# Memory rows of the weight gradients transposed inside their own stage, and the last 64 channels of two column groups computed side by side

## The chip, the cores and the metric

The kernel runs on one core of one Trainium2 chip, in one launch. The metric is the device time of that launch in microseconds (us), the median of several runs. The profile is one execution taken by the hardware profiler. PE is TensorE's matmuls, PEld its weight loads, DVE the vector engine, ACT the scalar engine, POOL GpSimd, SP the engine that only issues transfers. L79 is line 79 of the kernel, a helper that records all matmuls, so PE is read by tile names.

One measure is used throughout: the **stage**, the time from the end of the last matmul of the x gradients to the end of the span, read from each run's trace. Each stage time is that of one profile, and how well it repeats was not measured as such.

## The reference, cut to what matters

The reference is the forward pass and all gradients of a gated sum of two attentions: A, multi-query, and B, recurrent over 64 segments of 32 tokens with 8 memory rows.

```
def _B_ref(x, mem0, Wq, Wk, Wv, Wo, seg_len):       # x (1,2048,576), 32 heads of 128
    mem = mem0                                       # 8 rows
    for s in range(n_seg):                           # 64 segments
        h = concat([mem, x[segment s]])              # 8 + 32 rows
        q, k, v = h@Wq, h@Wk, h@Wv                   # per head
        o = softmax(mask(q k^T * scale)) v
        o = o @ Wo
        mem = o[:8]; outs.append(o[8:])
    return concat(outs)
...
_out, _vjp = jax.vjp(_f, ...)
return (_out, *_vjp(grad_out))
```

The last stage of the kernel forms the weight gradients of B: dWq, dWk and dWv (576 x 4096 each) are h^T times dq, dk, dv, and dWo (4096 x 576) is o^T times dy. The sum runs over 2560 rows: 2048 tokens and 64 x 8 = 512 memory rows, which is 16 + 4 blocks of 128. Of the 576 channels, four blocks have 128 and the fifth has 64.

## The kernel before: the parts that matter

The token rows of dq, dk, dv and o lie in DRAM in token order. The memory rows come out of the recurrence in another order, transposed, so a stage of its own turns them and writes them to DRAM:

```python
def b_mem_rows(self, sp, psum):
    for mt in range(self.NM // P):                     # 4 blocks x 4 sources
        for src, wi, dst in ((self.ME, 3, self.OM), (self.DME, 1, self.DM["q"]), ...):
            raw = sp.tile([P, 16, 256], BF16, name="m_raw", bufs=2)
            nc.sync.dma_start(raw[:], src[16 * mt:16 * mt + 16, :, wi, :]...)
            hm = sp.tile([P, HB, 16, MEM], BF16, name="m_hm", bufs=2)
            ...                                        # 16 copies bring the rows into order
            tk = sp.tile([P, 2, 4, 4, E], BF16, name="m_tk", bufs=2)
            for ri in range(8):
                self.tr4(psum, "x_tr", ..., tk[:, ri // 4, :, ri % 4, :])   # 4 transposes, 1 copy
            nc.gpsimd.dma_start(dst[mt * P:(mt + 1) * P, :], tk[:]...)
```

Then the weight gradient stage loads h, dy and one column group (512 of 4096 columns) after another, and multiplies:

```python
        def columns(xsrc, msrc, jc):
            t = sp.tile([P, NH, 512], BF16, name="w_col", bufs=2)
            for q in range(0, NTT, 4):
                (nc.sync if q % 8 == 0 else nc.gpsimd).dma_start(t[:, q:q + 4, :], xsrc[:, cs]...)
            nc.sync.dma_start(t[:, NTT:NH, :], msrc[:, cs]...)
            return t
        ...                                            # gate product, 32 matmuls
        for w, oi in (("q", 7), ("k", 8), ("v", 9)):
            for jc in range(8):
                t = columns(self.DX[w], self.DM[w], jc)
                for kt in range(NKT):                  # 5 channel blocks: 128,128,128,128,64
                    acc = psum.tile([P, 512], F32, name="w_acc", bufs=3)
                    for n in range(NH):                # 20 row blocks
                        self.mm(acc[0:rows, :], lhsT=h[:, n, kt * P:kt * P + rows], rhs=t[:, n, :], ...)
                    ...                                # copy to SBUF, store
        ...                                            # output gradient: 8 groups
```

The softmax here doesn't subtract the row's maximum and nothing guards it: scores larger than these inputs give would overflow.

## Time and profile before

| | before |
|---|---|
| median of 4 runs | 8813.72 us (8796.3 to 8819.1) |
| stage (end of x gradients to end) | 831.1 us |
| of that, until the first weight gradient matmul | 144.6 us |
| q, k, v gradients | 526.1 us |
| output gradient | 157.0 us |
| end | 3.5 us |

The page of the kernel before has the busy share of each engine, then the span in 40 equal slices of 220 us (a 9 is 90% or more; PEclk is the granted TensorE clock in tenths):

```profile
PE 8158.4 (93%) x89816; PEld 3903.5 (44%) x89816; DVE 4321.7 (49%) x6659; ACT 3835.0 (44%) x7412; POOL 1184.8 (13%) x3062
...
PEclk9999999999999989979999999989999877776999
DMA  2000000000000045542211588883333466666444
...
DMA packets 615950, 969.83 MB, mean 110 GB/s; under 512 B 187545, under 2 KB 406946, under 8 KB 594850
```

The stage is the last four slices.

### The profile page before, as it was taken

The numbers are of one execution on the slowest core, as the hardware profiler recorded it, in microseconds if no ns is written. First come the engines' busy times: TensorE is split into PE (matmuls) and PEld (weight loads), VectorE is DVE, ScalarE is ACT, GpSimd is POOL, SyncE is SP. The second block draws the span as 40 slices with busy tenths as digits, with TensorE's granted clock in tenths as the row PEclk, the third lists the DMA queues.
The fourth block names the chain that finished last, engine by engine and source line by source line (L and its number), as shares of the span: only waits on it lengthen the run. The fifth ranks groups of instructions, "written<-read, shape, count | busy, mean of one in ns | idle before, by whom it ended". The sixth has DMA issues, their size and how long they took to land. (4 is left out here: it accounts for less than half of the span.)

```text
span 8801.6 us, 210293 instructions
## 1 busy us (share of the span) xinstructions
PE 8158.4 (93%) x89816; PEld 3903.5 (44%) x89816; DVE 4321.7 (49%) x6659; ACT 3835.0 (44%) x7412; POOL 1184.8 (13%) x3062
## 2 busy tenths in 40 slices
PE   6999999999999979978999899979999799997999
PEld 2222222222222234435555566647777555554444
DVE  4889898898888924432333455542222111113000
ACT  3788787787777823332222355542222111112000
POOL 4100001000010014420000133320000011112000
PEclk9999999999999989979999999989999877776999
DMA  2000000000000045542211588883333466666444
GB/s 89 1 6 1 6 6 1 6 1 6 6 1 1 1 146 230 231 178 86 60 59 59 175 267 263 260 284 104 99 98 97 167 189 190 185 187 221 149 149 144
DMA packets 615950, 969.83 MB, mean 110 GB/s; under 512 B 187545, under 2 KB 406946, under 8 KB 594850
## 3 DMA queue, kind: packets, MB, share of 16 engines
q1 hardware_dynamic: 540978, 672.32, 24.4%
q0 software_dynamic: 72720, 282.73, 8.6%
q8 instruction: 702, 11.50, 0.5%
q14 instruction: 238, 1.95, 0.1%
q10 hardware_dynamic: 1312, 1.33, 0.0%
HBM read 552.06 MB, written 404.10 MB: 109 GB/s over the span
## 5 line engine op out<-in xcount | busy, mean ns | idle before, releaser
L1355 DVE TENSOR_TENSOR a_U<-a_d,a_E 128x1024 bf16<-128x1024 f32 x2048 | 2474.3, 1224 | 302.3 <-ACT a_E L1350 233.1
L1350 ACT ACTIVATE a_E<-a_s 128x512 bf16<-128x512 f32 x4096 | 2237.5, 595 | 564.7 <-PE a_s L79 478.9
L79 PE MATMUL a_s<-a_qaug,a_kmask 128*128 128x512 bf16 x2048 | 704.1, 388 | 54.7 <-ACT a_tk L1432 24.5
L79 PE MATMUL a_s<-a_kmask,a_qaug 128*128 128x512 bf16 x2048 | 697.3, 384 | 25.9 <-ACT a_E L1350 9.6
L79 PE MATMUL w_acc<-w_col,w_h 128*128 128x512 bf16 (+1 forms) x2400 | 526.1, 381 | 0.9 <-DMA w_col<-dqx 0.9
L79 PEld LDWEIGHTS <-d_g 128*32 128x32 bf16 x18432 | 494.6, 97 | 26.4 <-issue 9.9
L63 DVE CAST p_tok<-p_pb 128x512 bf16<-128x512 f32 x384 | 265.3, 692 | 318.4 <-PE p_pb L79 318.4
L79 PE MATMUL a_d<-a_doT,a_vaugT 32*128 32x512 bf16 x2048 | 401.5, 389 | 0.1
L79 PE MATMUL a_d<-a_vaugT,a_doaT 32*128 32x512 bf16 x2048 | 397.6, 385 | 0.0
L65 ACT COPY p_em<-p_tr 128x512 bf16<-128x512 bf16 x384 | 225.0, 586 | 357.7 <-PE p_tr L84 357.5
L1442 POOL TENSOR_TENSOR a_otok<-a_tk,a_rl 128x144 bf16<-128x144 f32 x64 | 27.5, 429 | 2525.4 <-DVE a_rl L1441 2525.4
L79 PEld LDWEIGHTS <-w_h 128*128 128x128 bf16 (+1 forms) x2400 | 237.4, 100 | 289.4 <-issue 24.2
L79 PEld LDWEIGHTS <-a_vaugT 32*128 32x128 bf16 x2048 | 96.4, 91 | 572.7 <-issue 572.6
L79 PEld LDWEIGHTS <-a_doaT 32*128 32x128 bf16 x2048 | 95.9, 91 | 538.0 <-issue 537.6
L65 ACT CAST c_tm<-c_pb 128x512 bf16<-128x512 f32 x192 | 112.5, 586 | 471.4 <-PE c_pb L79 471.2
L1042 ACT ACTIVATE g_dt<-x_p 128x512 bf16<-128x512 f32 x256 | 142.7, 599 | 355.5 <-DMA dvx<-g_dt 216.0
L63 DVE CAST c_tm<-c_pb 128x512 bf16<-128x512 f32 x192 | 132.9, 692 | 313.6 <-PE c_pb L79 309.2
L63 DVE CAST w_o<-w_acc 128x512 bf16<-128x512 f32 (+1 forms) x60 | 41.4, 690 | 481.3 <-PE w_acc L79 448.6
L79 PEld LDWEIGHTS <-c_mT 128*32 128x32 bf16 x7680 | 187.9, 96 | 190.9 <-DVE c_mT L396 25.4
L79 PEld LDWEIGHTS <-a_kmask 128*128 128x128 bf16 x2048 | 125.1, 97 | 313.8 <-issue 305.9
L79 PEld LDWEIGHTS <-p_xT 128*128 128x128 bf16 (+1 forms) x1920 | 154.8, 97 | 218.0 <-issue 87.7
L65 ACT CAST w_o<-w_acc 128x512 bf16<-128x512 f32 (+1 forms) x60 | 35.1, 585 | 496.6 <-PE w_acc L79 496.6
(482 smaller groups left out, 13797.5 us busy)
## 6 DMA issues: line engine op xcount, KB each, us to landing
xt_k<-p_tok SPq DMA_DIRECT2D x16, 1024.0 KB, 4.0
xe_k<-p_em POOLq DMA_DIRECT2D x16, 1024.0 KB, 5.5
xs_k<-p_seg POOLq DMA_DIRECT2D x64, 256.0 KB, 4.3
xt_v<-p_tok SPq DMA_DIRECT2D x16, 1024.0 KB, 3.9
xe_v<-p_em POOLq DMA_DIRECT2D x16, 1024.0 KB, 5.6
xs_v<-p_seg POOLq DMA_DIRECT2D x64, 256.0 KB, 2.9
xt_q<-p_tok SPq DMA_DIRECT2D x16, 1024.0 KB, 4.2
xe_q<-p_em POOLq DMA_DIRECT2D x16, 1024.0 KB, 5.8
```

The lines of the kernel that those rows point to most:

```text
L63: nc.vector.tensor_copy(out, in_)
L65: nc.scalar.copy(out, in_)
L79: self.follow(self.nc.tensor.matmul(out, lhsT, rhs, start=start, stop=stop, tile_position=tp, skip_group_check=True))
L1042: nc.scalar.mul(dt[:, g], pk[:], sc)
L1350: nc.scalar.activation(ex[:, j, :], s[:, :], ACT.Exp, scale=SCALEA)
L1355: nc.vector.tensor_tensor(out=u[:], in0=d[:], in1=ex[:], op=ALU.mult)
L1442: nc.gpsimd.tensor_tensor(out=osl, in0=v[:, :, :, o0:o0 + DA], in1=rl[:].to_broadcast([P, 4, 2, DA]), op=ALU.mult)
```

## The change

Its intent is to do away with the stage of memory rows: the raw rows are loaded to SBUF as they lie, four copies per column group bring them into order, and PE transposes them straight into the column group's buffer, inside the stage that PE bounds. At the same time the 64-channel block is done for two column groups at once, one in each half of the array. A third w_col buffer is needed for that, and everything is issued two groups ahead.

```diff
-    def b_mem_rows(self, sp, psum):          # the whole stage, its DRAM buffers and its call
 ...
+        def load_raw(w):
+            raw = raws[w] = sp.tile([P, self.NSEG, 256], BF16, name="w_raw", bufs=2)
+            for s in range(0, self.NSEG, 16):
+                nc.gpsimd.dma_start(raw[:, s:s + 16, :], src[s:s + 16, :, wi, :]...)
+        def columns(w, jc):
-            t = sp.tile([P, NH, 512], BF16, name="w_col", bufs=2)
+            t = sp.tile([P, NH, 512], BF16, name="w_col", bufs=3)
             for q in range(0, NTT, 4):
+                nc.sync.dma_start(t[:, q:q + 4, :], xsrc[:, cs]...)
-            nc.sync.dma_start(t[:, NTT:NH, :], msrc[:, cs]...)
+            hm = sp.tile([P, 4, self.NSEG, MEM], BF16, name="w_hm", bufs=2)
+            for i in range(4):
+                (nc.gpsimd if i == 3 else nc.vector).tensor_copy(hm[:, i], raws[w][:, :, c0:c0 + MEM])
+            for mt in range(NMT):
+                ptr = psum.tile([P, 4, P], BF16, name="w_tr", bufs=2)
+                for i in range(4):
+                    self.tr(ptr[:, i, :], hm[:, i, 16 * mt:16 * mt + 16, :]..., P)
+                nc.scalar.copy(t[:, NTT + mt, :], ptr[:]...)
 ...
+        load_raw("q")
+        t0 = columns("q", 0)
+        ...                                   # dy loads, rows of h and dy, then columns("q", 1)
+        def projection(od, jc, t, t2):
+            if jc % 2 == 0:                   # 64 channels of two column groups
+                acc = bank("w_acc64", 2)
+                for n in range(NH):
+                    for x, tx in enumerate((t, t2)):
+                        self.mm(acc[64 * x:64 * x + 64, :], lhsT=h[:, n, 512:D], rhs=tx[:, n, :], ..., tp=(0, 64 * x))
+            for kt in range(4): ...           # as before
 ...
+        for n, (w, jc) in enumerate(order):
+            if jc == 0 and w != "o":
+                load_raw("qkvo"["qkvo".index(w) + 1])
+            if n + 2 < len(order):
+                ts.append(columns(*order[n + 2]))
+            ...                               # projection or output of group n
+            if n == 0: gate()
```

The output gradient keeps its 1280 matmuls, but its last 64 columns go to a bank of their own.

More of the change, by code (lines that the diff above doesn't have):

```diff
@@ L176, in setup_dram @@
         self.OX = DT([T, J], "ox")
-        self.OM = DT([NM, J], "om")
     def load_B_fwd(self, pool):
@@ L773, in setup_dram_bwd @@
         self.DX = {"q": self.DQX, "k": DT([T, J], "dkx"), "v": DT([T, J], "dvx")}
-        self.DM = {w: DT([NM, J], f"dm_{w}") for w in "qkv"}
     def b_transpose_weights(self, sp, psum):
@@ L1055, in b_x_gradients @@
             nc.sync.dma_start(self.outs[1][tok, :], dx[:])
-    def b_mem_rows(self, sp, psum):
-        nc = self.nc
-        for mt in range(self.NM // P):
-            for src, wi, dst in ((self.ME, 3, self.OM), (self.DME, 1, self.DM["q"]), (self.DME, 2, self.DM["k"]), (self.DME, 3, self.DM["v"])):
-                raw = sp.tile([P, 16, 256], BF16, name="m_raw", bufs=2)
-                nc.sync.dma_start(raw[:], src[16 * mt:16 * mt + 16, :, wi, :].rearrange("s p n -> p s n"))
-                hm = sp.tile([P, HB, 16, MEM], BF16, name="m_hm", bufs=2)
-                for s in range(16):
-                    (nc.gpsimd if s % 2 else nc.vector).tensor_copy(hm[:, :, s, :], raw[:, s].rearrange("p (h m) -> p h m", m=MEM))
-                tk = sp.tile([P, 2, 4, 4, E], BF16, name="m_tk", bufs=2)
-                for ri in range(8):
-                    self.tr4(psum, "x_tr", lambda g: hm[:, 4 * ri + g].rearrange("p s m -> p (s m)"), tk[:, ri // 4, :, ri % 4, :])
-                nc.gpsimd.dma_start(dst[mt * P:(mt + 1) * P, :], tk[:].rearrange("p r g i e -> p (r g i e)"))
     def b_weight_gradients(self, keep, sp, psum):
@@ L1079, in b_weight_gradients @@
             nc.sync.dma_start(h[:, q:q + 4, :], self.A_x.rearrange("(n p) d -> p n d", p=P)[:, q:q + 4, :])
-            nc.sync.dma_start(dy[:, q:q + 4, :], self.db_dram[:, :].rearrange("(n p) d -> p n d", p=P)[:, q:q + 4, :])
         def rows_of(dst, hist, c0):
             for k4, n in ((0, 4), (4, 1)):
-                ptr = psum.tile([P, 4, P], BF16, name="w_tr", bufs=1)
+                ptr = psum.tile([P, 4, P], BF16, name="w_tr", bufs=2)
                 for k in range(n):
@@ L1090, in rows_of @@
                 self.evac(dst[:, k4 * P:k4 * P + w], ptr[:].rearrange("p k n -> p (k n)")[:, 0:w])
+        raws = {}
+        def load_raw(w):
+            src, wi = (self.ME, 3) if w == "o" else (self.DME, 1 + "qkv".index(w))
+            raw = raws[w] = sp.tile([P, self.NSEG, 256], BF16, name="w_raw", bufs=2)
+            for s in range(0, self.NSEG, 16):
+                nc.gpsimd.dma_start(raw[:, s:s + 16, :], src[s:s + 16, :, wi, :].rearrange("s p n -> p s n"))
+        def columns(w, jc):
+            xsrc = self.OX if w == "o" else self.DX[w]
+            t = sp.tile([P, NH, 512], BF16, name="w_col", bufs=3)
+            cs = slice(jc * 512, (jc + 1) * 512)
+            for q in range(0, NTT, 4):
+                nc.sync.dma_start(t[:, q:q + 4, :], xsrc[:, cs].rearrange("(n p) c -> p n c", p=P)[:, q:q + 4, :])
+            hm = sp.tile([P, 4, self.NSEG, MEM], BF16, name="w_hm", bufs=2)
+            for i in range(4):
+                c0 = ((jc // 4) * 16 + i * 4 + jc % 4) * MEM
+                (nc.gpsimd if i == 3 else nc.vector).tensor_copy(hm[:, i], raws[w][:, :, c0:c0 + MEM])
+            for mt in range(NMT):
+                ptr = psum.tile([P, 4, P], BF16, name="w_tr", bufs=2)
+                for i in range(4):
+                    self.tr(ptr[:, i, :], hm[:, i, 16 * mt:16 * mt + 16, :].rearrange("p s m -> p (s m)"), P)
+                nc.scalar.copy(t[:, NTT + mt, :], ptr[:].rearrange("p i n -> p (i n)"))
+            return t
+        load_raw("q")
+        t0 = columns("q", 0)
+        for q in range(0, NTT, 4):
+            nc.sync.dma_start(dy[:, q:q + 4, :], self.db_dram[:, :].rearrange("(n p) d -> p n d", p=P)[:, q:q + 4, :])
         for mt in range(NMT):
@@ L1097, in b_weight_gradients @@
         nc.sync.dma_start(self.outs[6].rearrange("b m d -> (b m) d"), dm0[0:MEM, :])
-        def columns(xsrc, msrc, jc):
-            t = sp.tile([P, NH, 512], BF16, name="w_col", bufs=2)
-            cs = slice(jc * 512, (jc + 1) * 512)
-            for q in range(0, NTT, 4):
-                (nc.sync if q % 8 == 0 else nc.gpsimd).dma_start(t[:, q:q + 4, :], xsrc[:, cs].rearrange("(n p) c -> p n c", p=P)[:, q:q + 4, :])
-            nc.sync.dma_start(t[:, NTT:NH, :], msrc[:, cs].rearrange("(n p) c -> p n c", p=P))
-            return t
+        bank = lambda name, bufs: psum.tile([P, 512], F32, name=name, bufs=bufs)
@@ L1107, in b_weight_gradients @@
         dz16 = keep.tile([P, NTT], BF16, name="w_dz16")
         nc.vector.tensor_copy(dz16[:], self.dz_all[:])
-        pg = psum.tile([P, 640], F32, name="w_acc2", bufs=2)
-        for lo, hi in ((0, 512), (512, D)):
-            for n in range(NTT):
-                self.mm(pg[0:1, lo:hi], lhsT=dz16[:, n:n + 1], rhs=h[:, n, lo:hi], start=(n == 0), stop=(n == NTT - 1))
         dg16 = keep.tile([1, D], BF16, name="w_dgate16")
-        nc.vector.tensor_copy(dg16[:, :], pg[0:1, 0:D])
-        nc.sync.dma_start(self.outs[11][None, :], dg16[:, :])
@@ L1116, in b_weight_gradients @@
-        for w, oi in (("q", 7), ("k", 8), ("v", 9)):
-            od = self.outs[oi].rearrange("d h e -> d (h e)")
-            for jc in range(8):
-                t = columns(self.DX[w], self.DM[w], jc)
-                for kt in range(NKT):
-                    rows = KT_ROWS[kt]
-                    acc = psum.tile([P, 512], F32, name="w_acc", bufs=3)
-                    for n in range(NH):
-                        self.mm(acc[0:rows, :], lhsT=h[:, n, kt * P:kt * P + rows], rhs=t[:, n, :], start=(n == 0), stop=(n == NH - 1))
-                    o16 = sp.tile([P, 512], BF16, name="w_o", bufs=3)
-                    self.evac(o16[0:rows, :], acc[0:rows, :])
-                    nc.sync.dma_start(od[kt * P:kt * P + rows, jc * 512:(jc + 1) * 512], o16[0:rows, :])
@@ L1128, in b_weight_gradients, with gate @@
-        oo = self.outs[10].rearrange("h e d -> (h e) d")
-        for jc in range(8):
-            t = columns(self.OX, self.OM, jc)
+        order = [(w, jc) for w in "qkvo" for jc in range(8)]
+        ts = [t0, columns(*order[1])]
+        def gate():
+            for lo, hi in ((0, 512), (512, D)):
+                pg = bank("w_acc", 4)
+                for n in range(NTT):
+                    self.mm(pg[0:1, 0:hi - lo], lhsT=dz16[:, n:n + 1], rhs=h[:, n, lo:hi], start=(n == 0), stop=(n == NTT - 1))
+                nc.vector.tensor_copy(dg16[:, lo:hi], pg[0:1, 0:hi - lo])
+            nc.sync.dma_start(self.outs[11][None, :], dg16[:, :])
@@ new lines, in projection @@
+        def projection(od, jc, t, t2):
[3 more added lines that the diff above has]
+                    for x, tx in enumerate((t, t2)):
+                        self.mm(acc[64 * x:64 * x + 64, :], lhsT=h[:, n, 512:D], rhs=tx[:, n, :], start=(n == 0), stop=(n == NH - 1), tp=(0, 64 * x))
+                o16 = sp.tile([P, 512], BF16, name="w_o", bufs=3)
+                self.evac(o16[:, :], acc[:, :])
+                for x in range(2):
+                    nc.sync.dma_start(od[512:D, (jc + x) * 512:(jc + x + 1) * 512], o16[64 * x:64 * x + 64, :])
+            for kt in range(4):
+                acc = bank("w_acc", 4)
+                for n in range(NH):
+                    self.mm(acc[:, :], lhsT=h[:, n, kt * P:(kt + 1) * P], rhs=t[:, n, :], start=(n == 0), stop=(n == NH - 1))
+                o16 = sp.tile([P, 512], BF16, name="w_o", bufs=3)
+                self.evac(o16[:, :], acc[:, :])
+                nc.sync.dma_start(od[kt * P:(kt + 1) * P, jc * 512:(jc + 1) * 512], o16[:, :])
@@ L1131, in b_weight_gradients, with output @@
+        def output(oo, jc, t):
+            a64 = bank("w_acc64", 2)
             for i in range(4):
-                acc = psum.tile([P, 640], F32, name="w_acc2", bufs=2)
+                acc = bank("w_acc", 4)
                 for n in range(NH):
-                    for lo, hi in ((0, 512), (512, D)):
-                        self.mm(acc[:, lo:hi], lhsT=t[:, n, i * E:(i + 1) * E], rhs=dy[:, n, lo:hi], start=(n == 0), stop=(n == NH - 1))
-                o16 = sp.tile([P, D], BF16, name="w_oo", bufs=3)
@@ L1137, in b_weight_gradients @@
-                self.evac(o16[:, :], acc[:, 0:D])
-                j0 = jc * 512 + i * E
-                nc.sync.dma_start(oo[j0:j0 + E, :], o16[:, :])
+                    lt = t[:, n, i * E:(i + 1) * E]
+                    self.mm(acc[:, :], lhsT=lt, rhs=dy[:, n, 0:512], start=(n == 0), stop=(n == NH - 1))
+                    self.mm(a64[:, 64 * i:64 * i + 64], lhsT=lt, rhs=dy[:, n, 512:D], start=(n == 0), stop=(n == NH - 1))
+                o16 = sp.tile([P, 512], BF16, name="w_o", bufs=3)
@@ new lines, in output @@
+                self.evac(o16[:, :], acc[:, :])
+                j0 = jc * 512 + i * E
+                nc.sync.dma_start(oo[j0:j0 + E, 0:512], o16[:, :])
+            o64 = sp.tile([P, 4, 64], BF16, name="w_o64", bufs=2)
+            self.evac(o64[:], a64[:, 0:256].rearrange("p (i c) -> p i c", i=4))
+            nc.sync.dma_start(oo[jc * 512:(jc + 1) * 512, 512:D].rearrange("(i p) c -> p i c", p=P), o64[:])
+        for n, (w, jc) in enumerate(order):
[3 more added lines that the diff above has]
+                ts.append(columns(*order[n + 2]))
+            if w == "o":
+                output(self.outs[10].rearrange("h e d -> (h e) d"), jc, ts[n])
+            else:
+                projection(self.outs[{"q": 7, "k": 8, "v": 9}[w]].rearrange("d h e -> d (h e)"), jc, ts[n], ts[n + 1])
+            if n == 0:
+                gate()
@@ L1649, in build_full @@
                     k.b_x_gradients(p5k, p5s, p5p)
-            with SB("p5m") as p5m, PS("p5mp") as p5mp:
-                k.b_mem_rows(p5m, p5mp)
             with SB("p6k") as p6k, SB("p6s") as p6s, PS("p6p") as p6p:
```

## The prediction

> **What bounds the kernel now.** I read the page first: PE is busy 93% of the span, but the slices just before the last three show DMA at 8 and a granted clock of 7. So I cut the end of the run into stages, with the busy time, the granted clock and the DMA share of each (columns: stretch, its length, busy us and instruction count of PE, PEld, DVE, ACT, POOL, then PEclk, DMA share, GB/s):
>
> ```profile
> 7970.50:8090.70 120.20, 68.84 (x516) 54.11 (x517) 54.30 (x194) 37.50 (x64) 53.31 (x144) 0.51 0.91 281
> 8090.70:8115.06 24.36, 14.95 (x73) 6.50 (x73) 4.46 (x11) 1.92 (x9) 3.02 (x4) 0.50 0.92 303
> 8115.06:8641.10 526.04, 526.04 (x2400) 237.32 (x2399) 41.38 (x60) 34.50 (x59) 34.36 (x46) 0.99 0.45 147
> 8641.10:8798.20 157.10, 157.02 (x1281) 80.63 (x1280) 12.12 (x16) 10.22 (x17) 10.46 (x14) 1.00 0.45 147
> ```
>
> The first row is the memory row stage. No engine is full, PE runs at half clock, and the DMA share is 0.91: transfers bound it. It lasts 120.2 us, from the last matmul of the x gradients to the landing of the last row block. The second row is the opening of the weight gradients, again transfers. The last two rows (q, k, v gradients, then the output gradient) are PE alone: 526.04 busy in 526.04 us at full clock, with transfers at half load. The chain of waits that ended last says the same of the seam:
>
> ```profile
> 8086.26 4.14 DMA dm_v<-m_tk
> ...
> 8093.07 15.63 DMA w_h<-in_A_x_dram
> ...
> 8110.19 0.37 SPq L1097
> 8110.56 0.06 issue
> 8110.61 4.41 DMA w_col<-dqx
> 8115.02 0.04 issue
> 8115.06 683.07 PE w_acc L79 x3680
> 8798.13 0.02 issue
> 8798.16 0.64 ACT w_oo L65
> ```
>
> Nothing of the last stage loads before the last row block lands (8090.40). Then h, and after it the first column group. L1097 is the small store of the memory gradient: SP takes its queue in order, so the first SP load of w_col stands behind it. From 8115.06 nothing but matmuls is on the path.
>
> **What the Trainium skill says.** (1) "TensorEngine Tiling (Array Packing)", When to Use Tiling: a stationary operand of 64 columns allows two column tiles, up to twice the rate. Its Key Properties add that a change of tiling mode drains TensorE. The trace of before supports the first with tiles of 32 columns (columns: start, us, what):
>
> ```profile
> 4401.95 1.05 PE L79 MATMUL c_pb<-Wq,c_mT 128*32 128x512 bf16 x16 [0.30 <-DVE c_mT L396]
> 4402.83 0.39 PE L79 MATMUL c_pb<-Wqk,c_mT 128*32 128x512 bf16 x4
> 4403.04 1.04 PE L79 MATMUL c_pb<-Wq,c_mT 128*32 128x512 bf16 x16
> ```
>
> Twenty matmuls of 512 columns pass from 4401.95 to 4403.04, 1.09 us: 0.218 us for each set of four. The drain is not seen on its own. (2) "TensorE: Matmul & The Clock Gate", Wait — 56ns, not 53.3ns?: 215.7 ns from start to start for 512 columns warm, 55.6 for 128. The trace agrees: 80 full matmuls in 17.38 us (217 ns), and the transposes below. (3) "DMA: Bandwidth & Descriptors", Queues, rings and completion order: an engine takes its queues in turn, a packet at a time. In before, POOL's w_col loads go in packets of 4096 B (four 1024 B rows that land side by side), SP's in 1024 B; median times 159 and 46 ns in the packet records. So where both queues have work, POOL gets most of the bytes.
>
> **The change part by part.** *Removed, transfers:* the memory rows are no longer written to DRAM in token order (16 stores of 1 MB) nor read back (32 loads of 512 KB), 33.6 MB less; the 16 raw loads of 1 MB stay, now from POOL. The 120.2 us stage goes as a stage.
>
> *Removed, PE:* the last 64 channels of q, k, v were 24 groups of 20 matmuls, each at full price for half the array. In steady state:
>
> ```profile
> 8226.81 16.95 PEld L79 LDWEIGHTS <-w_h 128*128 128x128 bf16 x80 [0.41 <-issue]
> 8244.19 4.02 PEld L79 LDWEIGHTS <-w_h 128*64 128x64 bf16 x20 [0.42 <-issue]
> 8248.62 16.95 PEld L79 LDWEIGHTS <-w_h 128*128 128x128 bf16 x80 [0.41 <-issue]
> ```
>
> 80 full ones take 17.38 us (8226.81 to 8244.19), 20 half ones 4.43. Before: 24 x 4.43 = 106.3 us. After: 12 sets of 20 pairs at 0.218 = 52.3, and I allow 1.7 for 24 changes of tiling. 54, so 52 us less.
>
> *Added, PE:* the transposes are the same 512 as before, but now stand in the PE-bound stage. At full clock:
>
> ```profile
> 7939.96 0.24 PEld L84 LDWEIGHTS <-g_me 128*128 128x128 bf16 x4
> 7940.16 0.27 PEld L84 LDWEIGHTS <-g_mde 128*128 128x128 bf16 x4
> 7940.38 0.10 PEld L79 LDWEIGHTS <-identB 128*128 128x128 bf16 x1
> ```
>
> Eight in 0.42 us, 53 ns each. 32 groups of 16; three are needed before the main loop, the other 464 cost 24.5 us on PE.
>
> *Added beside PE, hidden:* per group three DVE copies and one POOL copy to bring the rows into order (half that size took 219 and 391 ns), and four ACT copies of 586 ns. 128 x 0.586 = 75 us of ACT in a stage where ACT is busy 45 of 683 us.
>
> *Moved:* the gate product, 32 matmuls, from the opening into the stage: 16 x 0.217 + 16 x 0.03 = 4 us. The 1280 matmuls of the output gradient stay as they are (157.1 us); only their bank and their stores change.
>
> *The main stage then:* 1920 full matmuls x 0.2173 = 417; pairs 54; output 157; transposes 24.5; gate 4; sum 657 (before: 683). To this I add 14 us of bubbles, chosen, see rival 1.
>
> *The opening:* loads begin where the memory row loads began, at 7970.5. Before PE can run freely it needs h (2.36 MB), the first column group (2.1), the raw q rows (4.19) and the second group (2.1), because the pair reads two groups. dy (2.36) is ahead of the second group on SP, and raw k (4.19) is issued by POOL as soon as its q copies are done, so it takes the engines too. All: 17.3 MB. At 300 GB/s (281 and 303 in the two transfer-bound rows) that is 58 us; h, the first group and both raw loads alone, 12.8 MB, 43 us, after which four blocks of the first group could run if they stand ahead of the pair. I take 55 us, and 4 us for the end (3.4 now, and 128-byte rows in the last store).
>
> Sum from 7970.5: 55 + 657 + 14 + 4 = 730 us, against 8801.6 - 7970.5 = 831 now. That is 101 us less. From the median of 8812.75: about **8712 us**, 1.1% faster.
>
> **The rivals.** *1. The transposes stall PE.* w_tr has two buffers, and each is free again only after an ACT copy of 0.59 us. In the memory row stage exactly this is on the path (0.60 us of transposes, 0.59 of ACT, in turn). If PE's order has the 16 of a group in one block, it waits for two such copies, about 1.0 us beyond its 0.85: 29 x 1.0 = 29 us, time about 8727. For: the copy also waits for a w_col buffer that PE has only just released. Against: in the opening of before, gate matmuls stand between the w_tr transposes, so the order of PE does mix other work in. My 14 us is half of it.
>
> *2. The opening is no shorter than before.* If POOL's large packets starve h and the first group until both raw loads are in, and the second group stands behind the small store again, PE starts at 75 us or later: 8732. For: the packet sizes. Against: bytes are bytes, 17.3 MB have to pass either way. If instead PE works from 40 us on: 8697.
>
> *3. The column tiles give nothing* (the halves run one after the other): 106 instead of 54 us, 8764. The 0.218 us for four tiles speaks against it.
>
> *4. Transfers become the bound of the main stage.* It moves some 67 MB of columns, 12.6 of raw rows and 19 of stores in about 660 us, 150 GB/s, half of the 300 reached elsewhere. A column group of 2.1 MB has a full group of PE work (17.4 us) to land. I see no wait here.
>
> **Range and chances.** Optimistic on all (opening 42, bubbles 3): 706, that is 8688. Pessimistic (opening 75, bubbles 30, end 5): 767, that is 8749. I take 8682 to 8755. Two per cent is 176 us; the two old stretches together are only 144.6, and the pairs give 52, so over 2% faster would need an opening of almost nothing and free transposes. Slower by 2% would need a stall of over 270 us that I can't see. Faster 0.03, within 2% 0.96, slower 0.01.
>
> **What would show it.** Right: no stage of half-clock PE between the x gradients and the first w_acc longer than about 55 us; pairs of 128x64 at 0.22 us a pair; 1920 full matmuls still at 0.217; short idle time on PE before w_tr. Wrong: long PE waits named ACT (w_tr) or DMA (w_col) inside the stage, pairs at 0.43 us, or a first w_acc later than 8045. The least certain terms are the opening (15 us either way) and the bubbles.

## The result and the profile after

| | before | after |
|---|---|---|
| median | 8813.72 us (4 runs) | 8697.87 us (8691.55 to 8709.63, 4 runs) |
| stage | 831.1 | 724.2 |
| until the first weight gradient matmul | 144.6 | 11.3 |
| from there to the output gradient | 526.1 | 546.1 |
| output gradient | 157.0 | 163.0 |
| end | 3.5 | 3.8 |

The ratio is 0.9873, with a 95% interval of 0.9856 to 0.9891. A ratio is the mean time of one kernel's runs over that of the other's in the same rounds, so it is not quite the ratio of the medians. The same lines of the page of the kernel after:

```profile
PE 8017.3 (92%) x89332; PEld 3854.7 (44%) x89816; DVE 4302.5 (50%) x6562; ACT 3862.7 (44%) x7474; POOL 1124.3 (13%) x2902
...
PEclk9999999999999989988999999998999977777999
DMA  2000000000000035552111388875333266666443
...
DMA packets 596875, 936.25 MB, mean 108 GB/s; under 512 B 191001, under 2 KB 394018, under 8 KB 577826
```

33.6 MB less are moved, as predicted (16 stores and 32 loads of the memory rows). By the page PE is busy 141 us less, but 52 of these lie ahead of the stage, in the same code: there the trace of after lacks 409 matmul records (the page has 89332 matmuls for 89816 weight loads). In the stage itself PE is busy 89 us less, 677.8 instead of 766.9: the pairs take half the time, and part of what PE did before ran at half clock. The stage cut into opening, q/k/v gradients, output gradient and end (columns: stretch, its length, busy us and count of PE, PEld, DVE, ACT, POOL, then PEclk, DMA share, GB/s):

```profile
7965.50:8032.40 66.90, 29.54 (x177) 12.81 (x178) 10.05 (x24) 8.05 (x20) 11.92 (x12) 0.67 0.97 293
8032.40:8522.80 490.40, 486.61 (x2679) 230.30 (x2723) 64.36 (x128) 80.73 (x147) 26.50 (x32) 1.00 0.45 145
8522.80:8686.20 163.40, 161.69 (x1348) 85.77 (x1372) 16.56 (x32) 23.39 (x45) 3.00 (x4) 1.00 0.34 107
8686.20:8689.80 3.60, 0.00 (x0) 0.00 (x0) 0.56 (x1) 0.21 (x1) 0.00 (x0) 0.85 0.22 55
```

The half-clock stage of 144.6 us has become an opening of 66.9 us with a DMA share of 0.97, in which PE already does some of the products. The main part is PE alone again: 486.61 busy in 490.40 us, at full clock, with transfers at 0.45. Where the opening's time goes is in the timeline of PE's waits for transfers (in brackets: idle time before the line, and what ended it):

```profile
7976.87 2.42 PE L79 MATMUL w_acc<-w_col,w_h 128*64 128x512 bf16 x5 [11.34 <-DMA w_col<-dqx]
...
7985.17 1.86 PE L79 MATMUL w_acc<-w_col,w_h 128*128 128x512 bf16 x4 [5.88 <-DMA w_col<-dqx]
...
7993.69 1.86 PE L79 MATMUL w_acc<-w_col,w_h 128*128 128x512 bf16 x4 [6.66 <-DMA w_col<-dqx]
...
7999.25 4.84 PE L79 MATMUL w_acc<-w_col,w_h 128*128 128x512 bf16 x14 [3.69 <-DMA w_col<-dqx]
...
8019.75 0.64 PE L79 MATMUL w_acc<-w_col,w_h 128*64 128x512 bf16 x2 [9.49 <-DMA w_col<-dqx]
...
8032.39 8.15 PE L79 MATMUL w_acc<-w_col,w_h 128*128 128x512 bf16 x37
```

PE takes each quarter of the first group as it lands, and waits 11.3 + 5.9 + 6.7 + 3.7 = 27.6 us between them. Next in PE's order comes the pair, which needs the second group, and PE waits 9.5 us for it, until 8019.75. That is also a matter of PE's own order: the 37 full matmuls at 8032.39 need only the first group, 8.1 us of work until the gate product at 8040.47, and they stand behind the pair. Together the waits are 37.1 us. The chain of waits names what held the second group up, and then what stands on the path in the steady part:

```profile
7973.88 6.88 SPq L1105
7980.80 8.19 SPq L1105
7989.03 5.80 SPq L1105
7994.87 1.85 SPq L1105
7996.77 22.94 DMA w_col<-dqx
8019.75 0.64 PE w_acc L79 x2
...
8170.02 0.46 PE w_tr L84 x8
8170.54 0.60 ACT w_col L1099
8172.11 10.74 PE w_acc L79 x49
```

L1105 is the load of dy, which the output gradient alone needs, some 550 us later. SP issues its queue in order, so four dy loads (2.36 MB) stand ahead of the second group, and meanwhile POOL has loads of raw q and raw k (8.39 MB) in its own queue. This leaves three questions for experiments: what each part of the change is worth, whether the transposes cost more than PE time, and whether the opening is bound by the sum of its bytes or by their order.

### The profile page after: what moved, and what is told of

The parts are those of the page before. It is cut to its first block, busy times and chain, and to the rows that moved or that the text cites. A ratio compares the mean times of both kernels' runs of the same rounds, so it can differ in the third digit from the quotient of the medians.

```text
span 8689.8 us, 209445 instructions
## 1 busy us (share of the span) xinstructions
PE 8017.3 (92%) x89332; PEld 3854.7 (44%) x89816; DVE 4302.5 (50%) x6562; ACT 3862.7 (44%) x7474; POOL 1124.3 (13%) x2902
## 5 line engine op out<-in xcount | busy, mean ns | idle before, releaser
L79 PE MATMUL a_s<-a_qaug,a_kmask 128*128 128x512 bf16 x2048 | 700.5, 386 | 54.7 <-ACT a_tk L1464 24.5
L79 PE MATMUL w_acc<-w_col,w_h 128*128 128x512 bf16 (+1 forms) x2352 | 487.5, 383 | 40.1 <-DMA w_col<-dqx 37.1
L79 PEld LDWEIGHTS <-w_h 128*128 128x128 bf16 (+1 forms) x2400 | 212.5, 101 | 283.9 <-issue 48.9
```

The lines of the kernel that those rows point to most:

```text
L79: self.follow(self.nc.tensor.matmul(out, lhsT, rhs, start=start, stop=stop, tile_position=tp, skip_group_check=True))
```

## The experiments

Each was sent with runs of the kernel before on the same chip; "after" is the changed kernel. All gave correct results.

### What each part is worth: the pairs alone, the pairs left out, the rows through DRAM

The first kernel is the kernel before plus the pairs (and the third w_col buffer they need), memory rows through DRAM as before:

```diff
 # against the kernel before
+                if jc % 2 == 0: ...     # 20 pairs for groups jc and jc+1, tp=(0, 0) and (0, 64)
-                for kt in range(NKT):
+                for kt in range(4):
-            t = sp.tile([P, NH, 512], BF16, name="w_col", bufs=2)
+            t = sp.tile([P, NH, 512], BF16, name="w_col", bufs=3)
```

> The kernel before, with only the last 64 channels of two column groups side by side (w_col has three buffers for it; memory rows still through DRAM). Theory (the sum of the prediction): 24 groups of 4.43 us become 12 of about 4.4 us, so the stage is some 53 us shorter: 8760 us, ratio to before 0.994. Two halves should start within a few ns of each other, and a pair every 0.216 us. Rival: the gain comes from the memory rows alone and the pairs run in turn: no change, 8814.

Measured: 8761.42 us (8751.05 to 8775.73, 5 runs), ratio 0.9942 [0.9929, 0.9954]; stage 779.5, 51.6 below before. Its opening is 2.6 us longer (147.2 until the first product), the q/k/v part 54.2 us shorter. PE's weight loads in the steady part (start, duration, what):

```profile
8154.48 4.03 PEld L79 LDWEIGHTS <-w_h 128*64 128x64 bf16 x40 [0.42 <-issue]
8158.92 34.22 PEld L79 LDWEIGHTS <-w_h 128*128 128x128 bf16 x160 [0.41 <-issue]
8193.56 4.03 PEld L79 LDWEIGHTS <-w_h 128*64 128x64 bf16 x40 [0.42 <-issue]
```

Forty half-width matmuls pass in 8158.92 - 8154.48 = 4.44 us. Before, twenty took 4.43 us. So the second half of the array is free: the two halves of a pair start 3 to 4 ns apart. The change of width itself does cost something, but before as well as here: from a matmul with 128 columns of weights to one with 64, or back, it is 309 to 312 ns from start to start, against 216 within a run. The 0.42 and 0.41 us before the weight loads are these places. The pairs halve their number. Two groups take 39.08 us, against 2 x 21.81 = 43.62.

The second kernel is the changed one with the 64 channels of each group done alone:

```diff
-            if jc % 2 == 0:
-                ...                     # pairs of t and t2
+            acc = bank("w_acc64", 2)
+            for n in range(NH):
+                self.mm(acc[0:64, :], lhsT=h[:, n, 512:D], rhs=t[:, n, :], ...)
```

> The changed kernel with the last 64 channels of every column group alone, as before (same stationary block, one half of the array). Theory: 53 us longer than the changed kernel, 8751 us, all of it in the q, k, v part of the main stage, the opening at most 5 us different. Rival: the pairs in the changed kernel lose part of their gain because transposes break into them, then the difference is clearly below that of the pairs-only kernel (45 us or less).

Measured: 8757.48 us (8741.82 to 8761.77, 5 runs), ratio 0.9932 [0.992, 0.9945]; stage 766.3, so the pairs are worth only 42.1 us here, the figure that the rival named. Its reason is not the right one: in the steady part the pairs are worth 4.52 us in two groups here (46.30 - 41.78, table below) and 4.54 alone. The loss is in the opening. Against the 54.2 us of the q/k/v part when the pairs were alone, 12.1 are missing; the other 2.6 were not traced, but 9.5 of them are the wait for the second group, which this kernel doesn't have:

```profile
8005.03 1.89 PE L79 MATMUL w_acc<-w_col,w_h 128*64 128x512 bf16 x4 [11.34 <-DMA w_col<-dqx]
8013.57 1.87 PE L79 MATMUL w_acc<-w_col,w_h 128*64 128x512 bf16 x4 [6.66 <-DMA w_col<-dqx]
8022.09 2.40 PE L79 MATMUL w_acc<-w_col,w_h 128*64 128x512 bf16 x5 [6.65 <-DMA w_col<-dqx]
8027.39 4.91 PE L79 MATMUL w_acc<-w_col,w_h 128*64 128x512 bf16 x14 [2.90 <-DMA w_col<-dqx]
```

A pair ties two column groups together, and at the start of the stage that is paid for.

The third kernel is the changed one with the memory rows brought back to DRAM order in a stage of their own:

```diff
+            with SB("p5m") as p5m, PS("p5mp") as p5mp:
+                k.b_mem_rows(p5m, p5mp)
 ...
-            hm = ...; copies, transposes, ACT copies
+            nc.sync.dma_start(t[:, NTT:NH, :], msrc[:, cs]...)
```

> The changed kernel with the memory rows brought to token order in their own stage through DRAM, as before, pairs kept. Theory: the two parts of the change add up, so this one is 116 - 53 = 63 us slower than the changed kernel: 8761 us, with a stage of about 120 us at half clock, an opening of about 35 us after it and a main stage about 35 us shorter than in the changed kernel (no transposes). Rival: the parts do not add up, because the pair makes the opening wait for the second column group; then it is slower than 8775.

Measured: 8753.65 us (8749.37 to 8760.67, 5 runs), ratio 0.9932 [0.9919, 0.9944]; stage 769.6. Against the changed kernel that is 45.3 us more, not the 63 of the theory; the rival is false too. Against the pairs alone it is 9.9 us less. These 9.9 lie in the opening, where the order of the loads differs and the gate product has moved into the main part: the first product starts at 130.2 instead of 147.2 us, the part after it is 5.7 us longer and the end 1.4. Which of the two does it was not tried apart. So the stage's 106.8 us split along three kernels: **pairs 51.6, order of the opening 9.9, memory rows 45.3**. Taken in another order the parts differ, as the 42.1 us show. The last part is the balance of a removed stage of some 120 us, an opening that waits for raw rows, and the transposes on PE.

### Do the transposes cost more than PE time?

```diff
-                for i in range(4):
+                for i in (0, 1, 2, 3) * 2:
                     self.tr(ptr[:, i, :], hm[:, i, 16 * mt:16 * mt + 16, :]..., P)
```

> The changed kernel with each of the 512 memory row transposes done twice into the same place (same result). Theory: transposes cost PE 54 ns each and nearly all stand in the PE-bound stage: 480 x 54 ns = 26 us longer, 8724 us. Rival A: PE waits for the ACT copies of w_tr anyway, and the added transposes fit into that wait: 10 us or less. Rival B: each break in the matmuls costs more than its transposes, by waits that grow: 40 us or more.

Measured: 8731.21 us (8723.86 to 8738.88, 4 runs), ratio 0.9905 [0.989, 0.992]; stage 750.0, 25.7 us more for 512 more transposes, 50 ns each, as the theory had it (26) and neither rival. The steady part says it finer. The time from one set of pairs to the next, that is two column groups, is read from PE's weight loads; first the changed kernel, then this one:

```profile
8147.03 0.14 PEld L79 LDWEIGHTS <-w_h 128*64 128x64 bf16 x3
...
8188.83 0.35 PEld L79 LDWEIGHTS <-w_h 128*64 128x64 bf16 x5
```

```profile
8170.17 0.11 PEld L79 LDWEIGHTS <-w_h 128*64 128x64 bf16 x1
...
8213.51 0.11 PEld L79 LDWEIGHTS <-w_h 128*64 128x64 bf16 x1
```

| two column groups, steady part | us | transposes in them |
|---|---|---|
| before | 43.62 | 0 |
| pairs alone | 39.08 | 0 |
| after | 41.78 (mean of 41.76 and 41.80) | 32 |
| pairs left out | 46.30 | 32 |
| transposes twice | 43.34 | 64 |

The second 32 transposes cost 1.56 us, 49 ns each, the first 32 cost 41.78 - 39.08 = 2.70 us, 84 ns each. Neither is a transpose's own time: in a row they start 55 to 56 ns apart in all these kernels. So the second 32 partly filled gaps that were there already, and the first 32 cost 2.70 - 32 x 0.0556 = 0.92 us beyond their own time. Where that goes can be read from the steady part of the changed kernel:

```profile
8147.58 0.40 PE L84 MATMUL w_tr<-identB,w_hm 128*128 128x128 bf16 x4
8147.91 0.41 PE L79 MATMUL w_acc<-w_col,w_h 128*64 128x512 bf16 x2
...
8169.86 0.61 PE L84 MATMUL w_tr<-identB,w_hm 128*128 128x128 bf16 x8
8170.30 0.81 PE L79 MATMUL w_acc<-w_col,w_h 128*128 128x512 bf16 x3
8171.18 0.38 PE L84 MATMUL w_tr<-identB,w_hm 128*128 128x128 bf16 x4
```

Eight transposes between full matmuls take 0.44 us (8169.86 to 8170.30), but four between halves of pairs take 0.33 (8147.58 to 8147.91): the change to 64 columns. In two groups the transposes break into the pairs twice, which adds four changes of width, 0.09 to 0.12 us each, 0.40 together, and splits a pair, so that one half runs alone for 0.22. The three full matmuls at 8170.30 take 0.88 us until the next transpose instead of 0.65; there and at one more break PE waits for an ACT copy, 0.28 together. That is 0.90 of the 0.92. The kernel without pairs pays nearly the same (46.30 - 43.62 = 2.68), for it has 64-column matmuls that the transposes break into as well. These shares are read from one trace; the last experiment tries the part of ACT.

### The opening: bytes or order?

Three kernels move loads that could come later.

```diff
 # dy late: the dy loads go behind group 4
-        for q in range(0, NTT, 4):
-            nc.sync.dma_start(dy[:, q:q + 4, :], ...)
+            if n == 4:
+                ...                      # the same four loads
 # dy and raw k late: this, and
-            if jc == 0 and w != "o":
+            if jc == 2 and w != "o":
                 load_raw("qkvo"["qkvo".index(w) + 1])
 # raw q behind the first group (dy and raw k where the change has them)
+            if w == "q" and jc == 0:     # in columns, after its token loads
+                load_raw("q", nc.sync)
```

> The changed kernel, with the four loads of dy (2.36 MB, used only by the output gradient, 557 us later) taken out of the opening and issued at the fifth column group. Theory: in the changed kernel PE waits 9.5 us for the second column group before the first pair, and that group's loads stand behind dy on SP; so the stretch from the last matmul of the x gradients to the end of the span falls from 724.2 to about 715 us, and the wait before the first pair from 9.5 to under 1.5 us. Rival: raw k, issued by POOL just then, takes the bytes in place of dy, and the wait stays above 6 us: 721 or more.

> As the kernel with dy late, and the raw rows of k, v and o loaded at the third column group in place of the first. Theory (the waits of PE before the first pair are all that can be had from what comes after the first group): at most the same 9.5 us, 714 to 716 us from the x gradients to the end, and the three waits for the first group (16 us together) stay, since raw q still competes with it. Rival (the whole opening is bytes over rate, so 6.5 MB less saves 22 us): about 702 us.

> The changed kernel with the raw rows of q issued by SP behind h and the first column group, in place of POOL beside them. Theory 1 (POOL's large packets starve the first group): the first group lands by 16 us after the x gradients in place of 34, the three waits of 16 us before its blocks shrink to under 8 us, but the raw rows land later and PE then waits for them or for the second group, so 724 becomes 715 to 724. Theory 2 (only the sum of the bytes counts): 724 give or take 3, the waits only change places.

Measured:

| | median us (4 runs each) | ratio [95%] | stage | waits for transfers or raw rows, over 1 us |
|---|---|---|---|---|
| after | 8697.87 | 0.9873 [0.9856, 0.9891] | 724.2 | 11.3, 5.9, 6.7, 3.7, 9.5 |
| dy late | 8700.4 | 0.9873 [0.9857, 0.989] | 724.9 | 12.0, 5.9, 6.8, 3.0, 1.6, 7.0 |
| dy and raw k late | 8693.15 | 0.9865 [0.985, 0.988] | 715.8 | 15.3, 5.9, 6.6, 1.35 |
| raw q behind the first group | 8697.1 | 0.9871 [0.9856, 0.9886] | 717.3 | 11.6, 5.4, 6.6, 2.7 |

Moving dy alone brought nothing: the rival was right, raw k took the place of dy on the transfer engines, and the 9.5 us wait became one of 1.6 and one of 7.0. With raw k out of the way too, the wait for the second group shrinks to 1.35 us:

```profile
8007.80 5.05 PE L79 MATMUL w_acc<-w_col,w_h 128*128 128x512 bf16 x18 [0.29 <-DMA w_col<-dqx]
8014.43 0.38 PE L79 MATMUL w_acc<-w_col,w_h 128*64 128x512 bf16 x1 [1.35 <-DMA w_col<-dqx]
```

What is left are the waits for the quarters of the first group itself. The stage fell by 8.4 us, as the theory had it; the rival, that 6.5 MB less would save 22 us, is false. Raw k alone was not tried.

The third kernel landed in the range of its theory 1, but not for its reason: the three waits for the first group fell from 16.2 us to 12.6, not under 8. It did not test that reason either, for with raw q gone from POOL's queue, POOL issued raw k there 5.7 us into the stage (at 7975.54), beside the first group. What it does show is PE's order at work: here the blocks of the first group stand ahead of the pair, and although the second group was issued 45 us into the stage instead of 31, PE no longer waited for it.

The fourth kernel reorders the whole opening. h and the first group are loaded by turns, raw q behind them; the token blocks of the first group are multiplied first, into four open banks, and its memory blocks and the pair come last; dy and raw k stand late, raw k still on POOL.

```diff
+            for q in range(0, NTT, 4):           # first group only: h by turns with it
+                nc.sync.dma_start(h[:, q:q + 4, :], ...)
+                nc.sync.dma_start(t[:, q:q + 4, :], ...)
+        load_raw("q", nc.sync)
+        first = [bank("w_acc", 4) for kt in range(4)]
+        for kt in range(4):
+            for n in range(NTT):                 # 16 token blocks; 4 memory blocks follow later
+                self.mm(first[kt][:, :], lhsT=h[:, n, kt * P:(kt + 1) * P], rhs=t0[:, n, :], start=(n == 0), stop=False)
+        ...                                      # gate, then the copies and transposes of its memory rows
```

> The changed kernel with the opening in the order in which PE can use it: h and the first group chunk by chunk, raw q behind them on SP, the token parts of the first four blocks and the gate before any transposes, the first pair after those blocks, dy and raw k later. Theory: PE gets its first matmuls about 5 us after the x gradients and has 18 us of work while raw q lands; from the x gradients to the end 680 to 695 us in place of 724, so the kernel at about 8660. Rival (the bytes of h, first group and raw q, 8.65 MB, 29 us, bound the opening whatever the order): 700 to 710.

Measured: 8691.61 us (8676.97 to 8703.15, 4 runs), ratio 0.9863 [0.9847, 0.9878]; stage 708.0, 16.2 below the changed kernel but in the rival's range. What POOL issued tells why, and PE's waits show what it did:

```profile
7972.88 1.18 POOL L1080 DMA_DIRECT2D w_raw<-dme  x1 [18.71 <-DVE w_h L63]
7975.46 3.45 POOL L1080 DMA_DIRECT2D w_raw<-dme  x3 [1.40 <-issue]
```

```profile
7993.23 5.28 PE L79 MATMUL w_acc<-w_col,w_h 128*128 128x512 bf16 x15 [9.84 <-DMA w_col<-dqx]
8000.03 5.99 PE L79 MATMUL w_acc<-w_col,w_h 128*128 128x512 bf16 x27 [1.51 <-DMA w_col<-dqx]
...
8014.83 0.29 PE L84 MATMUL w_tr<-identB,w_hm 128*128 128x128 bf16 x1 [5.85 <-DVE w_hm L1101]
```

L1080 on POOL is raw k. Its place in the source is behind the copies for the first column groups on the same engine, but nothing that it needs comes from them, and it was issued 5.7 us into the stage, into the same transfer engines as raw q and the first group. The waits named DMA and DVE (whose copies wait for raw q) are the price. So the next kernel puts raw rows into SP's own order:

```diff
-        def load_raw(w, queue=nc.gpsimd):
+        def load_raw(w, queue=nc.sync):
```

> As the reordered opening of the run before this (its stage took 708.0 us, with waits of 9.8, 1.5 and 5.9 us in the first 30 us), but all raw loads of queries and keys are issued by SP, behind the column groups that are wanted first. Theory: in that run the raw keys' packets of 4096 bytes, issued early by POOL because nothing holds them back, took the transfer engines from the raw queries and the first group; standing last in SP's own order they can't. Then the stage takes about 694 us (680 to 700) and the kernel some 8675 us, 14 us below the run before and 22 below the changed kernel. Rival: the opening is limited by the sum of bytes, or by the stores of the x gradients that share SP's queue, and the order on SP matters little: 705 us or more, with the waits of the first 30 us still adding up to 15 us or more.

Measured: 8676.04 us (8670.09 to 8682.75, 5 runs), ratio 0.9845 [0.9832, 0.9859]; stage 693.7, as the theory had it (694). Of the three long waits one is left, and it is shorter:

```profile
7992.76 0.61 PE L79 MATMUL w_acc<-w_col,w_h 128*128 128x512 bf16 x1
7993.59 13.65 PE L79 MATMUL w_acc<-w_col,w_h 128*128 128x512 bf16 x61 [0.22 <-issue]
8007.17 2.12 PE L79 MATMUL w_acc<-w_h,w_dz 128*1 128x512 bf16 x16
8009.82 0.38 PE L79 MATMUL w_acc<-w_col,w_h 128*64 128x512 bf16 x1 [0.54 <-DVE w_dgate L1131]
8013.64 0.23 PE L84 MATMUL w_tr<-identB,w_hm 128*128 128x128 bf16 x1 [3.44 <-DVE w_hm L1101]
```

The gain over the fourth kernel, 14.3 us, is what the bytes say: raw k is 4.19 MB, and at the 293 GB/s that the transfers reached in this opening that is 14.3 us. So it is both: what is loaded ahead of or beside the urgent bytes costs its time, and order decides which bytes those are. Two things changed at once here, the place in the order and the packets (raw rows came in 4096 B on POOL's queue, in 512 B on SP's), so this run doesn't say whether packet size matters by itself.

### The copies of the transposed rows on two engines

```diff
 # against the kernel just above
-                nc.scalar.copy(t[:, NTT + mt, :], ptr[:]...)
+                self.evac(t[:, NTT + mt, :], ptr[:]..., use="sv"[mt % 2])     # ACT, DVE by turns
```

> As the run ahead of it, but the copies of the transposed memory rows from PSUM to SBUF alternate between ACT and DVE instead of all on ACT. Theory: the 0.6 us of an ACT copy that stands on the chain of waits at every odd column group costs time; with two engines the last copy of a group lands earlier, and the main part loses 3 to 7 us. Rival: the 0.6 us is only how the chain is followed, the matmuls wait for nothing there that counts, and the stage is within 2 us of the run ahead of it.

Measured: 8671.72 us (8665.1 to 8677.07, 4 runs), ratio 0.9839 [0.9826, 0.9853]; stage 688.7, 5.0 less, inside the theory's range. The medians differ by 4.3 us with ranges that overlap; the steady part is clearer: two groups take 41.52 us (41.48 and 41.55) instead of 41.78. So a wait for ACT was real, 0.26 us of the 0.92 us beyond the transposes' own time, close to the 0.28 read from the trace. The changes of width, and the pair that is split, are still there in this kernel; no run takes them away.

This is the fastest kernel: its stage is 35.5 us shorter than the changed kernel's and 142.4 shorter than before.

## Why the prediction was right

It said 8712 us in a range of 8682 to 8755, and within 2%; measured were 8697.87 us and a ratio of 0.9873. Its own sum stands term by term:

| term of the stage | predicted us | measured us | from |
|---|---|---|---|
| opening beyond the work counted below | 55 | 53.3 | what is left of 724.2 |
| full matmuls of q, k, v | 417 | 415.7 | 12 x (8193.56 - 8158.92), pairs alone |
| pairs | 54 | 53.3 | 12 x 4.44, pairs alone |
| output gradient | 157 | 157.0 | pairs alone |
| 464 transposes and bubbles | 24.5 + 14 | 37.1 | 368 x 0.0844, and 6.0 longer output gradient |
| gate | 4 | 4.0 | 8040.47 to 8044.49, after |
| end | 4 | 3.8 | after |
| sum | 730 | 724.2 | |

The first row is what the others leave, so the sum can't fail to fit. Read directly the opening is 53.6: 66.9 us until 8032.39, less what was done in it at the steady price, 41 full matmuls (8.9) and a set of pairs (4.4).

**The bound.** Half-clock memory row stage, transfer-bound opening, PE-bound rest: right, the stage as such went, and the rest is PE at clock 1.00. One reading was off without harm: the slice just before the last three shows DMA at 6 and a clock of 6, not 8 and 7; the stages were cut by windows.

**The pairs.** 52 us less was predicted; the q/k/v part became 54.2 us shorter when they alone were done. The Trainium skill's "TensorEngine Tiling (Array Packing)", Theoretical Speedup, says up to 2x for a dimension of at most 64, and this reaches it: 40 half matmuls in the time of 20. The prediction didn't see the drain on its own; the change of width costs 93 to 96 ns, in the kernel before too, and the 1.7 us allowed for it were about right: 53.3 measured against 240 x 0.2157 = 51.8 for the matmuls alone. Rival 3, no gain, is false. What the prediction did not see in its sum is that the pairs bring the 9.5 us wait for the second group; it did, however, list that group among the bytes of the opening, so the wait lies in the 55 us.

**The opening.** 55 us from 17.3 MB at 300 GB/s; 53.6 measured, 37.1 of it PE waiting, the rest mostly work at a granted clock of 0.67. The reason given, the sum of the bytes, holds in part: with dy and raw k away the stage fell by 8.4 us and not by 22; with the order changed as well it fell by 30.5. The prediction had also seen that blocks of the first group could run "if they stand ahead of the pair"; only half of them did. The worry that dy and raw k "take the engines too" was right; taking dy alone away was worth nothing. Rival 2, an opening no shorter than before, is false.

**Transposes.** The sum of 38.5 was near the 37.1 measured, but its second part by luck. At 55.6 ns each, as their starts in the traces have it, 464 transposes are 25.8 us (24.5 predicted) and the bubbles 11.3. The 14 us were chosen as half of rival 1, waiting for ACT copies, and of that only about 4 us were there (0.26 in two groups). The larger part is what the prediction did not have: transposes that break into the 64-column matmuls, each break with its changes of width. Rival 1 itself, 29 us, is false in size.

**Transfers in the main part.** 145 GB/s measured, 150 predicted, no wait named DMA there: rival 4 is false.

**The remaining 14 us.** The median was 14 us lower than predicted. The stage accounts for 5.8. The other 8 lie ahead of it, in code that the change doesn't touch: median less stage is 8813.7 - 831.1 = 7982.6 us before and 7973.7 after, and between 7975 and 7992 us in the other kernels. It is taken as scatter between runs, the luck of these four; no run isolates it.

## What to carry to other kernels

When a transfer-bound stage is folded into a PE-bound one, price the work that moves at PE's rate, and then look at the opening: what the new stage needs before its first product decides how much of the gain is kept. There, count the bytes that are ahead of or beside what is needed first, on all queues, and take every one of the unneeded loads away: removing dy alone let raw k take its place. Look at PE's order too: what needs the data that come last should stand last. A load that depended on nothing went out early here wherever it stood in the source, so put it behind the urgent ones in the same engine's queue.

## What the Trainium skill lacked or had wrong

- "TensorEngine Tiling (Array Packing)", Key Properties, says that a change of tiling mode drains TensorE and gives no price. Here each step between matmuls with 128 and with 64 columns of weights takes 309 to 312 ns from start to start, against 216 within a run, so 93 to 96 ns more. The 64-channel blocks of the kernel before, which give no tile position, pay the same, so these runs don't show that the tiling mode is the reason.
- No figure in what was read gives the price of mixing transposes with products. "TensorE: Matmul & The Clock Gate" has 55.6 ns for 128 columns, and transposes in a row start 55 to 56 ns apart here; but the 32 of two column groups cost 84 ns each. Of the excess of 0.92 us, 0.40 is changes of width, 0.28 waits for ACT, 0.22 a pair that was split.
- "DMA: Bandwidth & Descriptors", Queues, rings and completion order, says that an engine takes its queues in turn by packet, but not what share each then gets. In the opening of the changed kernel, from 7976 to 7992 us, POOL's queue moved 982 packets and SP's 1020, but 3.83 MB against 1.02: POOL's packets have 4096 B (median 219 ns), SP's mostly 1024 (61 ns). So the loads that were wanted first got the smaller part.
- No page that was read warns that a load with no dependency can be issued ahead of what the source puts before it on the same engine: raw k, written behind copies that POOL had to make first, went out 5.7 us into the stage. The kernel in which it did not, and in which its packets changed too, was 14.3 us faster.
